# ScalarE and VectorE in program order from the fourth plain step of a fused attention and two-layer MoE kernel

## The chip, the core and the metric

The kernel runs on one core of one Trainium2 chip. The metric is the device time of one execution in microseconds (us). Engines are named as the profile names them: PE (TensorE matmul), PEld (its weight loads), DVE (VectorE), ACT (ScalarE), POOL (GpSimd), SP (SyncE, which here issues DMAs only).

## The reference, cut to what matters

```python
def reference(q, k, v, w_in, w_out, w_gate, w_val, w_out2, rms_g):
    # B=4, H=8, S=576, D=64: local mask for heads 0-3, strided mask for heads 4-7
    x = attention(q, k, v).transpose(0, 2, 1, 3).reshape(2304, 512)
    h = x @ w_in                                # 512 -> 2048
    x = (h - np.tanh(h)) @ w_out                # 2048 -> 512      (MoE1)
    xn = x / np.sqrt(np.mean(x * x, -1, keepdims=True) + 1e-6) * rms_g
    g = xn @ w_gate                             # 512 -> 1536
    val = xn @ w_val
    return (g / (1 + np.exp(-g)) * val) @ w_out2    # 1536 -> 512  (MoE2)
```

The weights arrive as 64-bit floats. The kernel splits each into a high and a low 32-bit part and computes a product as three matmuls (high·high, high·low, low·high).

## The kernel before, in words

**Stages.** Attention runs first, with MoE1 overlapped; MoE1 goes through the 2304 tokens in five groups. Its last outputs stand in four accumulators `ps_x`; `evac_x` (L885) scales them on ACT into tiles `xe` (L890) and ACT's queue writes these to the DRAM tensor `x2d` (L896). MoE2 then treats the first R0 = 256 tokens in 12 "plain" steps (the loop at L1376, f = 0 to 11) and the other 2048 by Strassen products (class `Stage`, L1071), which need seven inputs `xt1` to `xt7`, built by `conv` (L1019) while the plain steps run. Everything asked about here lies in the plain steps and the some 10 us ahead of them.

**One plain step.** `pe_gv` (L923) runs 24 matmuls of 128x256 on TensorE: 12 for gate into a bank of PSUM, 12 for val into another. ACT takes silu of the gate (L937), VectorE multiplies by val (L938, tile `s`), ACT makes the high half of `p` (L940), VectorE the low half (L941). Two steps later `pe_o` (L944) multiplies `p` by w_out2: 6 matmuls of 128x512 into two accumulators `ps_x`. In every third step gate and val take two banks of the `ps_x` pool, in the others two of two banks tagged "h" and "m"; so three steps have banks at a time.

**Weights.** While the plain steps run, the last of w_gate and w_val are decoded. For one tile of 128x512: SP loads it (`raw`, L175, three buffers); ACT computes `ct` (L184) and `ca` (L186); VectorE merges them into `ct` (L196); ACT casts the high half `w` (L203); VectorE subtracts for the low half of `w` (L207). `Stream.step` (L230) does L184, L186, L196 for one weight and L203, L207 for the one before it. `Store.plain` (L338) stores merged tiles to DRAM (`v`, L343), `Store.to` (L346) the split ones. `Decode` on POOL later builds Strassen's weight combinations from `v` (L285, L302).

**Strassen inputs.** `conv(m)`: for m = 5, 6, 7, 4 VectorE first forms a difference `tr` (L1027); for m = 1, 2, 3 it needs none. Then ACT casts the high half (L1046) and VectorE subtracts for the low half (L1047). `preps` (L907) is a generator: it norms x, then yields one `conv` at a time.

**Order of the work.** A scheduler orders each engine's instructions with a timeline of its own, so the loop's program order is only a starting point; `tc.manual_schedule` makes the listed engines keep program order. Before, it holds for SP from MoE1's fourth group on, and for PE and SP after the plain steps. Each engine executes its list in that order.

## Time and profile before

| what | value |
|---|---|
| time, median of 3 runs | 887.31 us (885.79 to 887.9) |
| time of the profiled execution | 887.14 us |
| its span, first to last instruction | 885.3 us |
| mean granted TensorE clock | 0.990 |
| PE, DVE, ACT, POOL busy | 865.6, 626.1, 413.7, 247.6 us |
| the largest wait of PE between 455 and 545 us | 4.94 us, at 469.51 us |

The profiled execution takes 1.8 us more than its span. Times in the timeline count from the span's start. A matmul's busy time in the trace runs from its start to its modelled end, so a lone one shows more than the distance at which matmuls follow each other. In a view of instruction groups, "idle before" is the time in which the engine stood still just ahead of them, and the name behind the arrow is what ended it. The granted clock is 1.00 at 2.4 GHz and 0.50 at 1.2 GHz; a stretch with both shows a value between.

### The profile page before, as it was taken

What the parts mean: (1) busy time and instruction counts of PE and PEld (TensorE: products, weight loads), DVE (VectorE), ACT (ScalarE), POOL (GpSimd) and SP (SyncE); (2) the same over time, 40 slices, a digit from 0 to 9 for tenths busy, and PEclk for the clock granted to TensorE, in tenths of its full rate; (3) what the DMA queues carried; (4) which work ended last, traced back from release to release, by engine and by line L of the source; (5) the groups of instructions that cost most, each with busy time, mean ns of one, the idle gap of its engine ahead of it and who ended that gap; (6) DMA issues with size and microseconds to landing.
All of it is one profiled execution on the core that took longest, in us unless ns stands there. A gap on an engine that the chain in (4) does not pass through costs nothing.

```text
span 885.3 us, 14070 instructions
## 1 busy us (share of the span) xinstructions
PE 865.6 (98%) x5091; PEld 723.4 (82%) x5091; DVE 626.1 (71%) x1290; ACT 413.7 (47%) x916; POOL 247.6 (28%) x309
## 2 busy tenths in 40 slices
PE   7999999999999999999997999999999999999998
PEld 4888888888998887888887977888888888888886
DVE  5999778888779887657779845469688553435544
ACT  6887633323543333778657544533325324322230
POOL 0000057694366853000000449956200000000000
PEclk7999999999999999999999999999999999999999
DMA  9965224221313000889976889866661289544002
GB/s 302 367 221 180 76 75 157 98 63 36 116 55 110 25 19 26 330 311 366 412 262 226 302 304 410 329 239 214 212 216 48 82 315 348 182 147 140 1 1 95
DMA packets 63749, 164.12 MB, mean 185 GB/s; under 512 B 10112, under 2 KB 21760, under 8 KB 63680
## 3 DMA queue, kind: packets, MB, share of 16 engines
q1 hardware_dynamic: 62528, 162.18, 52.2%
q10 hardware_dynamic: 1152, 1.05, 0.3%
q8 instruction: 40, 0.66, 0.3%
q14 instruction: 29, 0.24, 0.1%
HBM read 119.16 MB, written 44.04 MB: 184 GB/s over the span
## 4 chain that ended last, share of the span: by engine, by line
PE 60%; DVE 9%; POOL 7%; issue 2%; DMA 2%; ACT 1%; ACTq 0%; SPq 0%; DVEq 0%; POOLq 0%
PE ps_pr L150 21%; PE ps_o L150 15%; PE ps_x L150 9%; PE ps_h L150 9%; POOL pr L674 5%; DVE so L714 4%; PE ps_q L150 4%; PE ps_m L150 1%; POOL pr L707 1%; DMA raw<-in_w_val_dram 1%; DVE tg L859 1%; DVE g L870 1%; DMA x2d<-xe 1%; DVE sm L450 0%; DMA sq<-in_q_str_dram 0%
## 5 line engine op out<-in xcount | busy, mean ns | idle before, releaser
L150 PE MATMUL ps_h<-xs,w 128*128 128x512 f32 (+1 forms) x984 | 214.3, 366 | 0.7 <-DVE tg L859 0.7
L150 PE MATMUL ps_x<-g,w 128*128 128x512 f32 (+1 forms) x984 | 214.1, 366 | 0.0
L150 PEld LDWEIGHTS ps_h<-xs,w 128*128 128x128 f32 x984 | 169.7, 190 | 30.5 <-DVE tg L859 1.2
L150 PEld LDWEIGHTS ps_x<-g,w 128*128 128x128 f32 x984 | 168.5, 189 | 30.3 <-ACT g L865 0.4
L150 PE MATMUL ps_pr<-xt,wt 128*128 128x512 f32 x576 | 137.0, 390 | 0.5 <-DVE s L1096 0.5
L150 PE MATMUL ps_o<-wt,p 128*128 128x512 f32 x576 | 135.9, 389 | 0.0
L150 PEld LDWEIGHTS ps_pr<-xt,wt 128*128 128x128 f32 x576 | 107.9, 188 | 23.6 <-DVE s L1096 0.9
L150 PEld LDWEIGHTS ps_o<-wt,p 128*128 128x128 f32 x576 | 108.1, 188 | 22.4
L674 POOL TENSOR_TENSOR pr<-sk,sq 128x256 f32<-128x256 f32 (+2 forms) x101 | 83.1, 857 | 132.2 <-DMA sq<-in_q_str_dram 127.8
L865 ACT CAST g<-tg 128x512 fp32r<-128x512 f32 (+1 forms) x82 | 46.5, 567 | 101.2 <-DVE tg L859 100.9
L1117 ACT COPY u<-ps_pr 128x512 f32<-128x512 f32 x72 | 41.9, 587 | 102.8 <-PE ps_pr L150 102.8
L707 POOL TENSOR_TENSOR pr<-sv,se 128x288 f32<-128x288 f32 (+12 forms) x104 | 69.7, 691 | 57.4 <-DVE so L714 19.8
L1169 DVE SCALAR_TENSOR_TENSOR osum<-ps_o,osum 128x512 f32<-128x512 f32 x80 | 54.8, 687 | 26.6 <-PE ps_o L150 25.9
L714 DVE TENSOR_REDUCE so<-pr 128x16 f32<-128x272 f32 (+11 forms) x104 | 64.8, 651 | 8.9 <-POOL pr L707 8.6
L302 POOL TENSOR_TENSOR ws<-wa 128x256 f32<-128x256 f32 x24 | 20.4, 872 | 179.6 <-DVE w L207 155.6
L150 PE MATMUL ps_pr<-xt,wo 128*128 128x512 f32 x288 | 67.4, 389 | 0.0
L150 PEld LDWEIGHTS ps_pr<-xt,wo 128*128 128x128 f32 x288 | 54.1, 188 | 11.2
L870 DVE TENSOR_TENSOR g<-tg,g 128x512 fp32r<-128x512 f32 (+1 forms) x82 | 55.2, 674 | 10.4 <-ACT g L865 9.8
L859 DVE SCALAR_TENSOR_TENSOR tg<-ps_h,tg 128x512 f32<-128x512 f32 (+1 forms) x82 | 50.5, 617 | 15.8 <-ACT tg L854 15.8
L196 DVE SCALAR_TENSOR_TENSOR ct<-ca,ct 128x512 uint32<-128x512 uint32 x68 | 47.5, 706 | 18.9 <-ACT ca L186 18.4
L854 ACT ACTIVATE tg<-ps_h 128x512 f32<-128x512 f32 (+1 forms) x82 | 44.2, 540 | 35.5 <-PE ps_h L150 35.4
L679 DVE TENSOR_REDUCE sc<-pr 128x4 f32<-128x256 f32 (+2 forms) x101 | 43.7, 436 | 12.1 <-POOL pr L674 11.6
(123 smaller groups left out, 1041.1 us busy)
## 6 DMA issues: line engine op xcount, KB each, us to landing
wt<-w SPq DMA_DIRECT2D x84, 512.0 KB, 4.6
w<-w SPq DMA_DIRECT2D x36, 512.0 KB, 6.2
raw<-in_w_out_dram SPq DMA_DIRECT2D x28, 512.0 KB, 6.1
w<-wo SPq DMA_DIRECT2D x24, 512.0 KB, 7.1
raw<-in_w_in_dram SPq DMA_DIRECT2D x16, 512.0 KB, 9.2
raw<-in_w_gate_dram SPq DMA_DIRECT2D x12, 512.0 KB, 7.0
raw<-in_w_val_dram SPq DMA_DIRECT2D x12, 512.0 KB, 7.4
v<-ct SPq DMA_DIRECT2D x24, 256.0 KB, 5.3
```

Source lines behind the costliest of these rows:

```text
L150: nc.tensor.matmul(out_, lhsT, rhs, start=start, stop=stop, skip_group_check=True)
L196: nc.vector.scalar_tensor_tensor(out=t, in0=self.a.bitcast(U32), scalar=3, in1=t, op0=ALU.logical_shift_left, op1=ALU.bitwise_or)
L674: nc.gpsimd.tensor_tensor(out=pr, in0=self.k[:, a:e, :], in1=self.q[:, c - c0:c - c0 + 1, :].to_broadcast([128, e - a, D]), op=ALU.mult,)
L679: pend.append(lambda: nc.vector.tensor_reduce(out=s[:, c - c0, a:e], in_=pr, axis=AX.X, op=ALU.add))
L707: nc.gpsimd.tensor_tensor(out=pr, in0=self.v[:, 0:c + 1, a:e], in1=self.e[:, c - c0, 0:c + 1].unsqueeze(2).to_broadcast([128, c + 1, e - a ...
L714: pend.append(lambda: nc.vector.tensor_reduce(out=o[:, c - g0, a:e], in_=pr.rearrange("l c d -> l d c"), axis=AX.X, op=ALU.add))
L854: nc.scalar.activation(out=t, in_=h_of[g, f, a], func=ACTF.Tanh, scale=WS)
L859: nc.vector.scalar_tensor_tensor(out=t, in0=h_of.pop((g, f, a)), scalar=WS, in1=t, op0=ALU.mult, op1=ALU.subtract)
L865: nc.scalar.copy(out=t[:, 0], in_=t_of[g, f, a])
L870: nc.vector.tensor_tensor(out=t[:, 1], in0=t_of.pop((g, f, a)), in1=t[:, 0].bitcast(F32), op=ALU.subtract)
L1117: nc.scalar.copy(out=u, in_=x[kd])
L1169: nc.vector.scalar_tensor_tensor(out=o, in0=ps, scalar=WS, in1=o, op0=ALU.mult, op1=ALU.add)
```

## The change

Five edits, all around the plain steps.

1. `Store.plain`: the eight `v` stores that come after MoE1 go to ACT's queue rather than SP's.
2. `evac_x` for the last group: the first two accumulators are moved into one pair tile of their own and stored together; the other two go to two tiles of another pool. Two stores of 128x2x256 and four of 128x256 take the place of eight of 128x256, and no tile is used twice.
3. `pe_gv`: gate and val of a step take the two halves of one bank, and six banks are taken in turn (two of "h", two of "m", two of the `ps_x` pool), so six steps have banks at a time.
4. The pools of the plain steps are opened in another order, so other buffers take over the memory that `xe` had.
5. From f = 3 to the loop's end ACT and VectorE keep program order. A step's order is: `Stream.step`s for its weights, the `v` stores, the matmuls, silu, `s`, `p`, then one Strassen input (two at f = 3, none before). Before, the generator was advanced three times a step from f = 0, and the scheduler placed what it issued.

```diff
@@ -340,7 +340,8 @@
                 w = w2[w2_order[self.m]]
                 if w.kind != "out2":
                     p, i = divmod(w.f, 2)
-                    nc.sync.dma_start(out=pairs[p].plain[2 * (w.kind == "val") + i], in_=w.b)
+                    queue = nc.sync if cvt.name == "cvt" else nc.scalar
+                    queue.dma_start(out=pairs[p].plain[2 * (w.kind == "val") + i], in_=w.b)
                 self.m += 1
 
         def to(self, n):
@@ -883,19 +884,32 @@
             evac_x(g)
 
     def evac_x(g):
-        queue = nc.sync if g < NG - 1 else nc.scalar
+        last = g == NG - 1
+        if last:
+            pair = ghl.tile([128, 2, 512], F32, tag="g0", name="xe")
         for c in range(4):
-            pool, tag = (gp, nth("tg", 3)) if g == NG - 1 else (cvt, ("ca", "ct")[c % 2])
-            t = pool.tile([128, 512], F32, tag=tag, name="xe")[:, :width[g]]
+            if last:
+                t = pair[:, c % 2] if c < 2 else gp.tile([128, 512], F32, tag=f"tg{c - 2}", name="xe")
+            else:
+                t = cvt.tile([128, 512], F32, tag=("ca", "ct")[c % 2], name="xe")[:, :width[g]]
             nc.scalar.mul(out=t, in_=xacc[g][c][:, :width[g]], mul=WS)
+            if last and c == 0:
+                continue
             for k, j in enumerate(groups[g]):
                 dst, src = x2d[c * 128:c * 128 + 128, :], t[:, SUB * k:SUB * k + SUB]
                 rs = runs(j)
                 b, t0, n, _ = rs[0]
-                if len(rs) == 1:
-                    queue.dma_start(out=dst[:, b * S + t0:b * S + t0 + n], in_=src)
+                if last and c == 1:
+                    nc.scalar.dma_start(
+                        out=x2d[:256, b * S + t0:b * S + t0 + n].rearrange("(c p) t -> p c t", p=128),
+                        in_=pair[:, :, SUB * k:SUB * k + SUB],
+                    )
+                elif last:
+                    nc.scalar.dma_start(out=dst[:, b * S + t0:b * S + t0 + n], in_=src)
+                elif len(rs) == 1:
+                    nc.sync.dma_start(out=dst[:, b * S + t0:b * S + t0 + n], in_=src)
                 else:
-                    queue.dma_start(
+                    nc.sync.dma_start(
                         out=dst.rearrange("p (b t) -> p b t", b=B)[:, :, t0:t0 + n],
                         in_=src.rearrange("p (b t) -> p b t", b=B),
                     )
@@ -922,11 +936,9 @@
 
     def pe_gv(j, f):
         r, n = [], R0
-        for kd, pool, tag in (("gate", ps_h, "h"), ("val", ps_m, "m")):
-            if f % 3 == 2:
-                ps = bank_x("ps_" + tag)[:, :n]
-            else:
-                ps = pool.tile([128, 512], F32, tag=nth(tag, 2), name="ps_" + tag)[:, :n]
+        bank = (bank_h, bank_m, bank_h, bank_m, bank_x, bank_x)[f % 6]("ps_h")
+        for k, kd in enumerate(("gate", "val")):
+            ps = bank[:, k * n:k * n + n]
             w, x = w2[kd, f].t, xn[j]
             seq = [(a, e, c) for c in range(4) for a, e in ((0, 0), (0, 1), (1, 0))]
             for i, (a, e, c) in enumerate(seq):
@@ -1366,28 +1378,33 @@
     for k, m in enumerate((3, 7)):
         xt[m] = late[:, 2048 * k:2048 * k + 4 * HT].rearrange("p (e c t) -> p e c t", e=2, c=2)
     poolB = ExitStack()
+    tmp[3] = (poolB.enter_context(tc.tile_pool(name="rawb", bufs=3, reuse_waits="tile")), "raw")
     tmp[0] = poolB.enter_context(tc.tile_pool(name="tmp", bufs=4, reuse_waits="tile"))
+    pb = poolB.enter_context(tc.tile_pool(name="pb", bufs=2, reuse_waits="tile"))
+    cvt = poolB.enter_context(tc.tile_pool(name="cvt2", bufs=2, reuse_waits="tile"))
     tmp[1] = None
-    cvt = poolB.enter_context(tc.tile_pool(name="cvt2", bufs=2, reuse_waits="tile"))
     tmp[2] = cvt
-    tmp[3] = (poolB.enter_context(tc.tile_pool(name="rawb", bufs=3, reuse_waits="tile")), "raw")
-    pb = poolB.enter_context(tc.tile_pool(name="pb", bufs=2, reuse_waits="tile"))
 
     for f in range(FB):
+        if f == 3:
+            order = ctx.enter_context(ExitStack())
+            order.enter_context(tc.manual_schedule(engines={mybir.EngineType.Activation, mybir.EngineType.DVE}))
         if f == FB - 4:
             pairs[0].fetch((0, 1))
         st2.to(max(3 * (f + 2), N1 + (len(w2_order) - N1) * (f + 1) // (FB - 2)))
         store.plain(st2.i - 1)
         store.to(st2.i - 6)
         pe_gv(0, f)
-        for _ in range(3 if f < FB - 2 else 40):
+        for _ in range((f >= 3) + (f == 3) if f < FB - 2 else 40):
             next(pg, None)
         decode.to(max(0, min(8, 8 * (f - 4) // 6)))
-        if f > 1:
+        if f >= 2:
             pe_o(0, f - 2)
-    pe_o(0, FB - 2)
+    for f in range(FB - 2, FB - 1):
+        pe_o(0, f)
     store.plain(len(w2_order))
     store.to(len(w2_order))
+    order.close()
     ctx.enter_context(tc.manual_schedule(engines={mybir.EngineType.PE, mybir.EngineType.SP}))
 
     def second():
```

What moves can be read from the instruction lists. Names carry the number of their buffer, and `p_5961` means the `p` of one step. **ACT, around the ninth gate weight, before:**

```order
L203 CAST w_5949<-ct_5939 128x512
L940 CAST p_5928<-s_5925 128x256
L940 CAST p_5984<-s_5981 128x256
L940 CAST p_6026<-s_6023 128x256
L184 ACTIVATE ct_6043<-raw_5937,colf_58 128x512
L186 ACTIVATE ca_6045<-raw_5937 128x512
L1046 CAST xt4_5708<-tr_5820 128x1024
L203 CAST w_5993<-ct_5944 128x512
L937 ACTIVATE s_6087<-ps_h_6061 128x256
L937 ACTIVATE s_6136<-ps_h_6110 128x256
L937 ACTIVATE s_6204<-ps_h_6178 128x256
L203 CAST w_6055<-ct_6043 128x512
```

The casts of weights stand close together, silu and `p` go in threes. **ACT, the same place, after:**

```order
L203 CAST w_5927<-ct_5917 128x512
L344 DMA v4_1_163<-ct_5917 128x512
L949 ACTIVATE s_5958<-ps_h_5933 128x256
L952 CAST p_5961<-s_5958 128x256
L1058 CAST xt5_5703<-tr_5964 128x1024
L203 CAST w_5974<-ct_5922 128x512
L344 DMA v4_3_165<-ct_5922 128x512
L949 ACTIVATE s_6003<-ps_h_5978 128x256
L952 CAST p_6006<-s_6003 128x256
L1058 CAST xt6_5704<-tr_6009 128x1024
L184 ACTIVATE ct_6027<-raw_5915,colf_58 128x512
L186 ACTIVATE ca_6029<-raw_5915 128x512
```

Behind gate 9's cast now come the silu and `p` of step f = 4, a Strassen cast of 128x1024, and only then the cast of val 9, `w_5974`. From the row of `ct_6027` the pattern begins anew: two steps f = 4 and f = 5 take one gate and one val weight, and so do f = 6 and 7, 8 and 9.

**VectorE, the same place, before:**

```order
L941 TENSOR_TENSOR p_5928<-s_5925,p_5928 128x256
L941 TENSOR_TENSOR p_5984<-s_5981,p_5984 128x256
L941 TENSOR_TENSOR p_6026<-s_6023,p_6026 128x256
L196 SCALAR_TENSOR_TENSOR ct_6043<-ca_6045,ct_6043 128x512
L1047 TENSOR_TENSOR xt4_5708<-tr_5820,xt4_5708 128x1024
L207 TENSOR_TENSOR w_5993<-ct_5944,w_5993 128x512
L938 SCALAR_TENSOR_TENSOR s_6087<-ps_m_6074,s_6087 128x256
L938 SCALAR_TENSOR_TENSOR s_6136<-ps_m_6123,s_6136 128x256
```

**VectorE, after:**

```order
L207 TENSOR_TENSOR w_5927<-ct_5917,w_5927 128x512
L950 SCALAR_TENSOR_TENSOR s_5958<-ps_h_5933,s_5958 128x256
L953 TENSOR_TENSOR p_5961<-s_5958,p_5961 128x256
L1039 TENSOR_TENSOR tr_5964<-x2_5239 128x1024
L1059 TENSOR_TENSOR xt5_5703<-tr_5964,xt5_5703 128x1024
L207 TENSOR_TENSOR w_5974<-ct_5922,w_5974 128x512
L950 SCALAR_TENSOR_TENSOR s_6003<-ps_h_5978,s_6003 128x256
L953 TENSOR_TENSOR p_6006<-s_6003,p_6006 128x256
L1039 TENSOR_TENSOR tr_6009<-x2_5239,tr_5964 128x1024
L1059 TENSOR_TENSOR xt6_5704<-tr_6009,xt6_5704 128x1024
L196 SCALAR_TENSOR_TENSOR ct_6027<-ca_6029,ct_6027 128x512
```

The low half of a weight had stood between Strassen's large instructions as its input came. Now the difference `tr_5964` follows the low half of `p_5961`, and the low half of the val weight `w_5974` and then `s_6003` follow the Strassen subtraction.

**TensorE, after, from the first matmuls of gate 9 (f = 9) to those of gate 10:**

```order
L150 MATMUL ps_h_6211<-xn_5193,w_5927 128x256 x12
L150 MATMUL ps_x_5846<-w_5325,p_5961 128x512 x2
L150 MATMUL ps_x_5847<-w_5325,p_5961 128x512 x2
L150 MATMUL ps_x_5846<-w_5325,p_5961 128x512
L150 MATMUL ps_x_5847<-w_5325,p_5961 128x512
L150 MATMUL ps_h_6211<-xn_5193,w_5974 128x256 x12
L150 MATMUL ps_x_5846<-w_5426,p_6006 128x512 x2
L150 MATMUL ps_x_5847<-w_5426,p_6006 128x512 x2
L150 MATMUL ps_x_5846<-w_5426,p_6006 128x512
L150 MATMUL ps_x_5847<-w_5426,p_6006 128x512
L150 MATMUL ps_h_6253<-xn_5193,w_6039 128x256 x12
```

Gate 10, val 10 and two more outputs follow in the same pattern, so that from gate 9's first matmul to gate 11's first there are 48 of 128x256 and 24 of 128x512; the outputs in between are those of steps 4 to 7. Ahead of these rows, from the end of MoE1's matmuls on, TensorE's list has 168 of 128x256 (steps 1 and 3 to 8) and 24 of 128x512 (the outputs of steps 0 to 3), so it runs four to five steps ahead of its outputs; before, three.

## Rows read from the trace of the kernel before

**Rows 1.** The page: span, and busy time of each engine.
```profile
span 885.3 us, 14070 instructions
...
PE 865.6 (98%) x5091; PEld 723.4 (82%) x5091; DVE 626.1 (71%) x1290; ACT 413.7 (47%) x916; POOL 247.6 (28%) x309
```

**Rows 2.** What TensorE waits for, 455 to 545 us; columns as in the second row.
```profile
engine line waited for: us in total, times, longest us
PE ps_h L150 <- ACT s L937: 4.9, 1, 4.9
PE ps_x L150 <- ACT p L940: 1.0, 1, 1.0
PE ps_pr L150 <- DVE s L1096: 0.5, 1, 0.5
PE ps_m L150 <- ACT w L203: 0.3, 1, 0.3
PE ps_m L150 <- DVE w L207: 0.2, 1, 0.2
```

**Rows 3.** Timeline of TensorE around 470 us; columns as in the second row.
```profile
start us, us, engine line op out<-in xcount [idle before <-releaser]
...
460.40 1.35 PE L150 MATMUL ps_m<-xn,w 128*128 128x256 f32 x10
461.59 2.91 PE L150 MATMUL ps_x<-g,w 128*128 128x512 f32 x12
464.34 0.40 PE L150 MATMUL ps_m<-xn,w 128*128 128x256 f32 x2
...
466.47 3.04 PE L150 MATMUL ps_m<-xn,w 128*128 128x256 f32 x24
474.45 3.74 PE L150 MATMUL ps_h<-xn,w 128*128 128x256 f32 x18 [4.94 <-ACT s L937]
```

**Rows 4.** Stretches of 5 and 10 us: busy time by engine, granted clock, DMA share.
```profile
core 0: us, PE busy (x) PEld busy (x) DVE busy (x) ACT busy (x) POOL busy (x), PEclk, DMA share, GB/s
...
470.00:475.00 5.00, 0.55 (x2) 0.55 (x3) 4.90 (x9) 2.84 (x7) 0.00 (x0) 0.90 0.17 59
475.00:480.00 5.00, 5.00 (x35) 5.00 (x34) 4.78 (x7) 5.00 (x7) 0.00 (x0) 0.75 0.49 161
480.00:485.00 5.00, 5.00 (x40) 4.82 (x40) 5.00 (x7) 5.00 (x10) 0.00 (x0) 1.00 0.96 320
...
500.00:510.00 10.00, 10.00 (x66) 9.11 (x65) 6.25 (x8) 3.88 (x9) 9.11 (x11) 1.00 0.99 346
```

**Rows 5.** Timeline of ScalarE, 467 to 475 us.
```profile
467.76 0.33 ACTq L896 DMA_DIRECT2D x2d<-xe  x1
468.13 0.60 ACT L890 ACTIVATE xe<-ps_x 128x512 f32<-128x512 f32 x1 [2.21 <-DMA x2d<-xe]
468.76 1.05 ACTq L896 DMA_DIRECT2D x2d<-xe  x2
472.16 0.76 ACT L184 ACTIVATE ct<-raw,colf 128x512 uint32<-128x512 uint16 x1 [3.43 <-DMA x2d<-xe]
472.82 0.66 ACT L186 ACTIVATE ca<-raw 128x512 f32<-128x512 f32 x1
473.38 0.75 ACT L184 ACTIVATE ct<-raw,colf 128x512 uint32<-128x512 uint16 x1
474.03 0.90 ACT L937 ACTIVATE s<-ps_h 128x256 f32<-128x256 f32 x3
```

**Rows 6.** ScalarE's groups by shape, 470 to 530 us: busy, mean ns, idle before.
```profile
L184 ACT ACTIVATE ct<-raw,colf 128x512 uint32<-128x512 uint16 x10 | 7.5, 766 | 9.2 <-DMA raw<-in_w_val_dram 5.0 <-DMA x2d<-xe 3.4 <-DMA raw<-in_w_gate_dram 0.5
L186 ACT ACTIVATE ca<-raw 128x512 f32<-128x512 f32 x10 | 6.6, 664 | 0.0
L203 ACT CAST w<-ct 128x512 fp32r<-128x512 f32 x10 | 6.2, 617 | 3.7 <-DVE ct L196 3.6
L940 ACT CAST p<-s 128x256 fp32r<-128x256 f32 x12 | 4.5, 404 | 7.5 <-DVE s L938 5.5 <-PE ps_x L150 1.8
L1046 ACT CAST xt<-tr 128x1024 fp32r<-128x1024 f32 x4 | 4.1, 1039 | 0.0
L937 ACT ACTIVATE s<-ps_h 128x256 f32<-128x256 f32 x12 | 3.8, 370 | 0.0
```

**Rows 7.** VectorE's groups by shape, same stretch.
```profile
L207 DVE TENSOR_TENSOR w<-ct,w 128x512 fp32r<-128x512 f32 x10 | 8.5, 854 | 1.4 <-ACT w L203 1.4
L196 DVE SCALAR_TENSOR_TENSOR ct<-ca,ct 128x512 uint32<-128x512 uint32 x10 | 7.5, 749 | 4.9 <-ACT ca L186 4.9
L941 DVE TENSOR_TENSOR p<-s,p 128x256 fp32r<-128x256 f32 x12 | 6.3, 560 | 1.2 <-ACT p L940 1.2
L1047 DVE TENSOR_TENSOR xt<-tr,xt 128x1024 fp32r<-128x1024 f32 x4 | 4.8, 1210 | 0.0
L938 DVE SCALAR_TENSOR_TENSOR s<-ps_m,s 128x256 f32<-128x256 f32 x12 | 4.5, 412 | 2.6 <-PE ps_m L150 2.6
...
L1027 DVE TENSOR_TENSOR tr<-x 128x1024 f32<-128x1024 f32 x2 | 2.4, 1214 | 0.0
```

**Rows 8.** Timeline of VectorE, 489 to 496 us, before POOL runs.
```profile
489.17 1.21 DVE L1047 TENSOR_TENSOR xt<-tr,xt 128x1024 fp32r<-128x1024 f32 x1
490.31 0.68 DVE L207 TENSOR_TENSOR w<-ct,w 128x512 fp32r<-128x512 f32 x1
490.91 0.68 DVE L196 SCALAR_TENSOR_TENSOR ct<-ca,ct 128x512 uint32<-128x512 uint32 x1
491.51 1.07 DVE L938 SCALAR_TENSOR_TENSOR s<-ps_m,s 128x256 f32<-128x256 f32 x3
...
495.45 1.08 DVE L941 TENSOR_TENSOR p<-s,p 128x256 fp32r<-128x256 f32 x3
```

**Rows 9.** Timeline of ScalarE at the end of the plain steps.
```profile
515.87 0.77 ACT L184 ACTIVATE ct<-raw,colf 128x512 uint32<-128x512 uint16 x1 [3.22 <-DMA raw<-in_w_val_dram]
```

## The prediction

> **What bounds the kernel now.** I read the page first: TensorE is busy 865.6 of 885.3 us [rows 1], so a change here can only take away waits of TensorE or add some. The view of its waits shows where they are: between 455 and 545 us five, 6.9 us in sum, 4.94 of them one stall [rows 2]. The timeline of TensorE gives its place, 469.51 us, and its sequel: the 18 matmuls of 128x256 behind it took 3.74 us, where 24 took 3.04 us before it [rows 3]. The stretches give the reason: the granted clock was 0.90 and then 0.75, so for part of the time at the lower of the two levels, and again 1.00 from 480 us [rows 4]. At full clock these matmuls follow each other every 0.119 us (ten from 460.40 to 461.59) and those of 128x512 every 0.229 us (twelve from 461.59 to 464.34) [rows 3]; 18 x 0.119 plus a tail of 0.18 us (3.04 less 24 x 0.119) is 2.32 us, so the clock cost 1.42 us.
>
> TensorE waited for a silu, and ScalarE's timeline shows why that was late: an `xe` eviction waited 2.21 us and a `ct` 3.43 us, both for a store of `xe` to `x2d`, with the three silus behind them in the list [rows 5].
>
> **The change part by part.**
>
> *Evictions and pools (edits 2 and 4).* Each of the four `xe` has a place of its own, and the next pools' first tiles do not lie where `xe` was. Both waits of [rows 5] lose their cause; what remains on ScalarE is four evictions of 0.60 us and six DMA issues of 0.33 to 0.5 us. *Banks (edit 3).* With six steps' banks TensorE does not ask for silu 0 after three steps, but its list goes on with step 1 and most of step 6 (46 matmuls of 128x256, 5.5 us) ahead of the first output. Either part takes the 4.94 us and the 1.42 us away. The small waits near 519 to 522 us, 0.3 + 0.2 + 1.0 = 1.5 us [rows 2], also go or are replaced by what comes below; the 0.5 us for `s` of L1096 I leave where it is, since it belongs to Strassen's first product. Gain: 4.9 + 1.4 + 1.5 = 7.8 us, the most that these rows hold.
>
> *The `v` stores on ScalarE (edit 1).* Eight issues of some 0.4 us (0.33 for one, 1.05 for two, [rows 5]) move from SP's queue to ScalarE's; their cost is in the chain below. SP loses as much, but its loads of `raw` wait for free buffers, so I count nothing there.
>
> *Program order (edit 5).* This is the part that costs. From f = 3 on each instruction of ScalarE and VectorE waits for all that stand ahead of it in the list. I followed the printed lists with the durations of the trace. An instruction of ScalarE starts about 0.1 us before its forerunner's end (`ca` 0.66 us after a `ct` of 0.76 [rows 5]), so in a row `ct` takes 0.66, `ca` 0.56, a weight's cast 0.52, a Strassen cast 0.95 us, from means of 0.766, 0.664, 0.617 and 1.04 [rows 6]; silu 0.37, `p` 0.40 and an issue 0.40 stand in full. VectorE takes 0.68 for a merge or a weight's low half and some 0.41 for `s` or the low half of `p` while POOL rests [rows 8], 1.21 for a difference or a Strassen subtraction [rows 7]. Hand-overs between engines I take at 0.04 us.
>
> - Step f = 4: `ct`, `ca`, `ct`, `ca`, cast, issue: 0.66 + 0.56 + 0.66 + 0.56 + 0.52 + 0.40 = 3.4. Then silu, `s` on VectorE, `p`: 1.25. Then ScalarE has nothing to do until VectorE has made the low half of `p` and the difference: 0.41 + 1.21 + hand-overs = 1.7. Then the Strassen cast, 0.95. Sum 7.2 us (rounded down).
> - Step f = 5: the cast of val 9, issue and silu hide under VectorE, which has the Strassen subtraction of step 4 (1.21), the low half of val 9 (0.68) and `s` (0.41) to do: `p` can start 2.3 us after the cast of val 9 does. Then 0.40 + 1.7 + 0.95. Sum 5.3 us.
> - Step f = 6: as f = 4, but its Strassen input needs no difference: 7.2 - 1.7 = 5.5 us. Step f = 7: as f = 5, 5.3 us.
>
> From the low half of gate 9 (step f = 4) to that of gate 11 (at the same place of step f = 8) that is 7.2 + 5.3 + 5.5 + 5.3 = **23.3 us**. TensorE's own work between the first matmuls of these two gates is 48 x 0.119 + 24 x 0.229 = **11.2 us**. If it comes to gate 9 no later than this weight, it stands 12.1 us in sum. Does it? MoE1's matmuls end near 466 us, as before (the last twelve `ps_x` end near 464.5 [rows 3], a few more stand behind them); 168 x 0.119 + 24 x 0.229 = 25.5 us later it is 491.6. On ScalarE: evictions from 465.5, their issues to 470.5, three silus (one waits for step 1's matmuls, 466.2 + 48 x 0.119 = 471.9) and three `p` to 474.0, two `ct` and `ca` for step 7's weights to 476.4, a wait of some 1.7 for VectorE, which ends the norm of x first, two casts and two issues to 480.0; step f = 3 with two Strassen casts 8.0, to 488.0; then the four decodes and the cast of gate 9, 3.0, and its low half 0.7: 491.8 us. So both come at once, and none of the 12.1 us is covered. They fall on val 9 and gates 10 and 11, about 2, 4 and 4 us with the matmuls at lower clock in between; val 11 comes 5.3 us after gate 11, for which TensorE has 12 matmuls of gate 11, 12 of Strassen's first products and an output of six: 1.4 + 4.1 = 5.5 us, just enough.
>
> *The clock.* In this trace it fell after a wait of 4.94 us and not after one of 1.0 us [rows 2, 4]. Between them no row tells. The two stalls of 3.5 to 4 us are nearer to the first, so I take the fall for both: one is within the 12.1 us (it delays TensorE's way to gate 11, and the weights don't care), the other adds 1.4 us. Bounds: nothing is added if it doesn't fall after the last, and 2.8 if that fall lasts twice as long.
>
> Sum: -7.8 + 12.1 + 1.4 = **+5.7 us** against the profiled execution's 887.14, which is 0.2 under the median: **892.8 us**. 0.3% is 2.7 us, about what a measurement of this kernel can tell from no change: slower.
>
> One rule is weighed here. What the row shows: a `ct` that waited 3.43 us for a store held back three silus [rows 5], two of whose banks TensorE had filled before. The Trainium skill says the same of these engines in general ("TensorE: Matmul & The Clock Gate", Architectural detail): ScalarE and VectorE are strict first-in, first-out queues. By this the bubbles above (1.7 at f = 4, 5 and 7, some 1.0 at each odd step for `s`, and 0.9 to 1.3 for `s` at each even one) are paid by all behind them, 23.3 us in sum. Were ready instructions let past, the four steps would take ScalarE's own work alone, 14.8 us (3.4 + 0.3 + 0.3 + 0.95, and 0.52 + 0.4 + 0.3 + 0.3 + 0.95, both twice), TensorE would stand 3.6, and the sum would be -7.8 + 3.6 = -4.2 us, 882.9. The row decides for the queue.
>
> **The rivals.**
>
> *The chain keeps pace (faster).* If the four steps took 11.2 us or less per TensorE's need, or TensorE came to gate 9 later than I think, only the gain stays: 887.14 - 7.8 = 879.3 us; with half of the 12.1 us covered and no fall of the clock, 885.4. It decides at 19.0 us for the four steps instead of 23.3 (7.8 + 11.2); below 16.3 the kernel is faster by over 0.3%. For it: before, both engines did the same work in this stretch with waits of TensorE of 1.5 us, and ScalarE is busy only 3.88 of 10 us from 500 to 510 us [rows 4]; TensorE is released earlier. Against it: the list lets no work be moved into these idle times, and VectorE's 1.21 us instructions stand on ScalarE's way five times in the four steps (three differences, two subtractions). The Trainium skill speaks for this rival ("Perfetto Trace Analysis", Matmuls): independent matmul groups should rotate through different PSUM banks so that one's evacuation overlaps the next's matmuls. No stall of the rows for banks alone is left for that after 480 us, though.
>
> *About even.* Half of the bubbles are hidden, or the clock stays up and VectorE's work is a little shorter: 885 to 889.8 us.
>
> *A weight comes late from DRAM (slower still).* ScalarE's last val weight waited 3.22 us for its load [rows 9], with the DMA engines busy 0.99 of the time [rows 4]. In the fixed list a late `raw` holds back silu, `p` and the Strassen input as well, and a `v` store that waits on ScalarE's queue does so too. One such wait in the chain adds 3.2 us: 896.0. VectorE is dearer beside POOL: 0.854 and 0.560 us for the low halves of weight and `p` [rows 7] rather than 0.68 and 0.41, which adds 0.15 x 4 + 0.17 x 4 = 1.3 us to the chain.
>
> *The change does not do what it says.* The printed lists show the program order and the six banks, so this has no chance worth a number.
>
> **How the numbers follow.** Forecast (890 to 894.5) 0.50; slower still 0.10; about even 0.14; faster 0.26, of which some 0.10 below 881. So faster 0.26, same 0.14, slower 0.60. The range leaves out the best tenth of the faster case and what lies above a late weight with its dearer VectorE (892.8 + 3.2 + 1.3 = 897.3): 881 to 897. The forecast's own range is 890 (no second fall of the clock, -1.4, and a chain shorter by 6 in 100, another -1.4) to 894.5 (VectorE dearer beside POOL, +1.3, and rounding).
>
> **What would show it.** Right: the stall of 4.94 us and the fall of the clock at 474 us gone; new stalls of TensorE between 494 and 515 us, of 3 us and more, in matmuls of `ps_h` for `w` of L207 on VectorE; ScalarE waiting for VectorE's `tr` about 1.7 us ahead of four Strassen casts; the plain steps ending some 5 us later. Wrong: no stall above 1 us after 480 us, or the old stall still there, or the stalls waiting for `raw` rather than for `w`.

## The result, and the profile after

| | before | after |
|---|---|---|
| median, runs of this comparison | 886.63 us (4 runs) | 898.36 us (897.02 to 899.84, 4 runs) |
| span of the profiled execution | 885.3 us | 897.1 us |
| mean granted clock | 0.990 | 0.986 |

The ratio is 1.012, with a 95% interval of 1.0096 to 1.0145: slower by 10.6 us, 8.5 to 12.9 (the two medians are 11.7 us apart, the two profiled executions 11.8). The direction was forecast; the size was not, and the time lies above the range.

The page of the changed kernel, as in [rows 1]:

```profile
span 897.1 us, 14054 instructions
...
PE 869.2 (97%) x5091; PEld 725.0 (81%) x5091; DVE 634.2 (71%) x1290; ACT 413.3 (46%) x916; POOL 247.6 (28%) x309
```

TensorE's waits between 440 and 600 us, as in [rows 2], the two largest groups:

```profile
engine line waited for: us in total, times, longest us
PE ps_h L150 <- ACT w L203: 8.8, 3, 4.1
PE ps_h L150 <- DVE w L207: 3.3, 3, 2.1
```

Its timeline, as in [rows 3], shows each of them; the wait in brackets lies ahead of the row's first matmul:

```profile
495.21 0.50 PE L150 MATMUL ps_h<-xn,w 128*128 128x256 f32 x2 [1.03 <-ACT w L203]
496.55 2.43 PE L150 MATMUL ps_h<-xn,w 128*128 128x256 f32 x10 [0.84 <-DVE w L207]
...
505.03 0.80 PE L150 MATMUL ps_h<-xn,w 128*128 128x256 f32 x2 [4.10 <-ACT w L203]
507.93 2.50 PE L150 MATMUL ps_h<-xn,w 128*128 128x256 f32 x10 [2.10 <-DVE w L207]
...
519.84 0.50 PE L150 MATMUL ps_h<-xn,w 128*128 128x256 f32 x2 [3.65 <-ACT w L203]
520.66 2.50 PE L150 MATMUL ps_h<-xn,w 128*128 128x256 f32 x10 [0.32 <-DVE w L207]
```

The stall at 469.5 us is gone. Six new waits, 12.0 us in sum, stand at val 9, gate 10 and gate 11, where the forecast had put 12.1 us. The stretches, as in [rows 4], add what the forecast had not:

```profile
core 0: us, PE busy (x) PEld busy (x) DVE busy (x) ACT busy (x) POOL busy (x), PEclk, DMA share, GB/s
...
475.00:480.00 5.00, 5.00 (x35) 4.59 (x34) 4.39 (x8) 3.00 (x6) 0.00 (x0) 1.00 0.89 293
...
495.00:500.00 5.00, 3.95 (x15) 3.52 (x16) 3.42 (x6) 1.95 (x5) 0.91 (x2) 0.67 0.99 269
500.00:505.00 5.00, 0.93 (x4) 0.39 (x2) 3.23 (x3) 3.00 (x6) 4.92 (x6) 0.84 0.98 397
505.00:510.00 5.00, 2.87 (x11) 2.57 (x12) 4.22 (x5) 1.96 (x4) 4.92 (x5) 0.50 1.02 407
510.00:515.00 5.00, 5.00 (x23) 4.38 (x22) 4.47 (x5) 0.86 (x3) 4.92 (x6) 0.63 0.82 316
...
520.00:525.00 5.00, 4.68 (x19) 4.11 (x20) 3.36 (x6) 2.32 (x5) 0.00 (x0) 0.66 0.37 134
```

TensorE now runs through 475 to 480 us at full clock, but from 495 us on the granted clock falls again and again. A value of 0.67 over 5 us is 3.3 us at the lower level; the five low rows make 17 us, where the kernel before had 3.5 us in all of the plain steps ((1 - 0.75) x 2 x 5 + (1 - 0.90) x 2 x 5 from [rows 4]).

ScalarE's timeline gives the chain, since the casts of gate 9, val 9, gate 10, val 10 and gate 11 are the rows at 489.76, 494.54, 504.37, 509.56 and 519.18:

```profile
489.76 0.60 ACT L203 CAST w<-ct 128x512 fp32r<-128x512 f32 x1
...
494.54 0.61 ACT L203 CAST w<-ct 128x512 fp32r<-128x512 f32 x1
...
503.15 0.76 ACT L184 ACTIVATE ct<-raw,colf 128x512 uint32<-128x512 uint16 x1 [2.00 <-DMA w<-w]
...
504.37 0.61 ACT L203 CAST w<-ct 128x512 fp32r<-128x512 f32 x1
...
508.30 0.41 ACT L952 CAST p<-s 128x256 fp32r<-128x256 f32 x1 [3.04 <-DVE s L950]
...
509.56 0.61 ACT L203 CAST w<-ct 128x512 fp32r<-128x512 f32 x1
...
519.18 0.60 ACT L203 CAST w<-ct 128x512 fp32r<-128x512 f32 x1
```

VectorE's low halves of gates 9 and 11 start at 490.50 and 519.92, **29.4 us** apart, not 23.3:

```profile
490.50 0.69 DVE L207 TENSOR_TENSOR w<-ct,w 128x512 fp32r<-128x512 f32 x1
...
501.52 1.21 DVE L196 SCALAR_TENSOR_TENSOR ct<-ca,ct 128x512 uint32<-128x512 uint32 x1
504.50 1.70 DVE L196 SCALAR_TENSOR_TENSOR ct<-ca,ct 128x512 uint32<-128x512 uint32 x1 [1.77 <-ACT ca L186]
506.13 1.75 DVE L207 TENSOR_TENSOR w<-ct,w 128x512 fp32r<-128x512 f32 x1
507.80 0.41 DVE L950 SCALAR_TENSOR_TENSOR s<-ps_h,s 128x256 f32<-128x256 f32 x1
...
513.47 2.31 DVE L1039 TENSOR_TENSOR tr<-x 128x1024 f32<-128x1024 f32 x1
...
519.92 0.68 DVE L207 TENSOR_TENSOR w<-ct,w 128x512 fp32r<-128x512 f32 x1
```

POOL ran from 499.09 us, and its last row of that stretch ends at 516.9:

```profile
499.09 1.43 POOL L302 TENSOR_TENSOR ws<-wa 128x256 f32<-128x256 f32 x2 [157.17 <-PE ps_h L150]
...
513.24 3.68 POOL L286 TENSOR_TENSOR wo<-ws,wo 128x512 fp32r<-128x512 f32 x2
```

Beside POOL two merges of 128x512 took 1.21 and 1.70 us where they take 0.69 without it, the low half of gate 10 1.75 and not 0.68, a Strassen difference 2.31 and not 1.21. `s`, which has one input in PSUM, stays at 0.41.

### The profile page after: what moved, and what is told of

It reads as the page before. It is cut to its first block, busy times and chain, and to the rows that moved or that the text cites. A ratio compares the mean times of both kernels' runs of the same rounds, so it can differ in the third digit from the quotient of the medians.

```text
span 897.1 us, 14054 instructions
## 1 busy us (share of the span) xinstructions
PE 869.2 (97%) x5091; PEld 725.0 (81%) x5091; DVE 634.2 (71%) x1290; ACT 413.3 (46%) x916; POOL 247.6 (28%) x309
## 4 chain that ended last, share of the span: by engine, by line
PE 48%; DVE 12%; POOL 7%; DMA 7%; ACT 4%; issue 3%; SPq 0%; ACTq 0%; DVEq 0%; POOLq 0%
PE ps_pr L150 20%; PE ps_o L150 14%; POOL pr L675 5%; PE ps_x L150 5%; PE ps_h L150 5%; DVE so L715 4%; PE ps_q L150 4%; DMA w<-w 2%; DMA raw<-in_w_val_dram 2%; DMA raw<-in_w_out_dram 1%; POOL pr L708 1%; ACT ct L184 1%; DVE tg L860 1%; ACT ca L186 1%; DVE g L871 1%
## 5 line engine op out<-in xcount | busy, mean ns | idle before, releaser
L150 PEld LDWEIGHTS ps_pr<-xt,wo 128*128 128x128 f32 x288 | 54.1, 188 | 11.2
L150 PE MATMUL ps_h<-xn,w 128*128 128x256 f32 x288 | 41.9, 303 | 12.0 <-ACT w L203 8.8
```

The lines of the kernel that those rows point to most:

```text
L150: nc.tensor.matmul(out_, lhsT, rhs, start=start, stop=stop, skip_group_check=True)
```

## The experiments

Eighteen kernels. Since the first 400 us of a profiled execution differ from run to run by up to 5 us (the 2900th matmul, ahead of all that was changed, starts between 402.3 and 407.3 us), traces are compared by TensorE's n-th matmul, counted from 0: its start less that of the 2900th, against the same in the kernel before. Minus is a lead. A ratio below is always to the kernel before, run in the same comparison, with its 95% interval. Worked out from the matmul rows of each trace:

```
matmul  before  after   e1    e2     e4    e6    e9    e15   e17
3240    478.9   -6.0   -6.3  +0.3   -5.9  -6.4  -5.9  -6.5  -6.5
3320    490.4   -6.0   -6.3  +0.9   -5.9  -6.4  -5.9  -6.0  -6.0
3400    502.0   -6.7   -0.8  +0.5   -6.3  -5.0  -6.6  -4.3  -4.5
3440    508.1   +6.8   -1.1  +1.1   +3.1  -4.9  +2.8  -4.3  -4.2
3480    515.4  +12.4   -1.2  +8.6   +7.0  +0.4  +3.2  -3.6  +2.0
3560    533.5  +11.3   -1.6  +8.2   +7.0  -0.1  +9.9  -3.4  +3.9
5090    881.3  +13.1   -0.7 +10.2   +7.5  +1.9 +10.7  -1.8  +4.9
```

The order of the two shapes of matmul differs between the kernels, so at some rows a kernel has done more or less work than the one before: at 0.119 and 0.229 us each the difference is up to 2.0 us (e2 at the 3480th; 1.2 for the changed kernel there). At the 2900th, 3240th, 3560th and 5090th matmul all kernels have done the same work, and at the 3320th the changed kernel has too.

The changed kernel has a lead of 6 us until 494 us and loses 17.3 us between the 3320th and the 3560th matmul. Its waits there are 12.04 us against 1.49 before: 10.55 of the 17.3. The rest, some 6.7 us, I put down to the lower clock: of the 17 us at that level TensorE worked for about 13, and ten matmuls of 128x256 took 2.43 us there (row 496.55) where they had taken 1.35 at full clock [rows 3].

### The order, and POOL beside it (e1 to e4)

My theory after the result: the fixed order's chain is the cause as forecast, and VectorE beside POOL made it longer. Rivals: the other edits, or the order only together with them.

**e1**, the change without edit 5:

```diff
-        if f == 3:
-            order = ctx.enter_context(ExitStack())
-            order.enter_context(tc.manual_schedule(engines={mybir.EngineType.Activation, mybir.EngineType.DVE}))
...
-    order.close()
...
-        for _ in range((f >= 3) + (f == 3) if f < FB - 2 else 40):
+        for _ in range(3 if f < FB - 2 else 40):
```

> The changed kernel without its fifth edit: the scheduler orders ScalarE and VectorE, three Strassen inputs are offered a step from f = 0, the other four edits stay. Theory (the program order alone is what costs): the stall of 4.94 us and the fall of the clock stay gone, no new stall over 1.5 us comes in their place, 879 to 883 us. Rival (the one-bank steps, the pools or the v stores on ScalarE's queue cost): stalls of 3 us and more between 490 and 525 us stay, 893 us or more.

Measured: 887.35 us, ratio 1.0001 (0.9987 to 1.0014). Edit 5 is what costs, and the other four edits gain nothing in sum, which I had not expected. The table shows why: their 6.3 us are there at 485 us and most of them are given back by 502. TensorE's timeline and the stretches (columns as above) of e1:

```profile
494.68 1.80 PE L150 MATMUL ps_h<-xn,w 128*128 128x256 f32 x12 [1.82 <-DVE w L207]
```

```profile
480.00:490.00 10.00, 9.65 (x67) 8.64 (x65) 10.00 (x13) 10.00 (x17) 0.00 (x0) 1.00 0.80 292
490.00:500.00 10.00, 7.82 (x41) 6.75 (x41) 10.00 (x17) 7.11 (x14) 3.58 (x2) 0.83 1.02 331
```

VectorE is busy 10.00 of 10 us in both stretches. TensorE comes sooner to weights that come no sooner (counted from the 2900th matmul, seven low halves in a row start 2.3 to 3.5 us later than before), waits 1.82 us for one, and loses more to the clock that falls behind it (0.83).

**e2**, the kernel before with edit 5 alone (against before):

```diff
+        if f == 3:
+            order = ctx.enter_context(ExitStack())
+            order.enter_context(tc.manual_schedule(engines={mybir.EngineType.Activation, mybir.EngineType.DVE}))
...
-        for _ in range(3 if f < FB - 2 else 40):
+        for _ in range((f >= 3) + (f == 3) if f < FB - 2 else 40):
...
+    order.close()
```

> The kernel before with the fifth edit alone (program order from f = 3 and one Strassen input a step). Theory: the old stall of 4.94 us stays and the chain of the fixed order comes on top, with gate 11's low half some 25 to 29 us behind gate 9's: 895 to 905 us. Rival (the order costs only together with six banks or the stores on ScalarE): within 3 us of before.

897.65 us, ratio 1.0116 (1.0095 to 1.0137), as expected. Its first stall stays, at 5.25 us, and a second of 5.78 us comes at 518 us.

**e3**, val weights split a step earlier:

```diff
-        st2.to(max(3 * (f + 2), N1 + (len(w2_order) - N1) * (f + 1) // (FB - 2)))
+        st2.to(max(3 * (f + 2), N1 + (len(w2_order) - N1) * (f + 1) // (FB - 2)) + (f in (4, 6, 8)))
```

> The changed kernel, with the split of val 9, 10 and 11 one step earlier (steps f = 4, 6 and 8), so that their casts stand ahead of silu, p and the Strassen input. If the place of the val weights' cast behind a Strassen input is what costs: the waits of TensorE ahead of val weights (1.9, 2.1 and 0.3 us) go and those ahead of gates 10 and 11 shrink too, about 888 us. If the length of the whole chain from gate to gate is what costs: the val waits go, but gates 10 and 11 still come 12 and 14 us apart, and the waits move to them: 894 to 898 us.

900.24 us, ratio 1.014 (1.0124 to 1.0156). The waits for val are gone, those for gates 10 and 11 grew to 5.2 and 6.3 us, and a wait of 2.34 us for a `p` came in: it is the chain's length that counts. The time lies above what either theory gave.

**e4**, POOL's work out of the way (the combinations and their loads come behind the last step; POOL starts at 514 us):

```diff
-        decode.to(max(0, min(8, 8 * (f - 4) // 6)))
+        decode.to(8 if f == FB - 1 else 0)
```

> The changed kernel, with POOL's decode of the first pair (and its loads) issued at the last plain step rather than from f = 5 on. If VectorE beside POOL and the loads in SP's queue made the chain longer than I had summed (29.4 us from gate 9's to gate 11's low half instead of 23.3): it comes down to 23 to 25 us, and the waits for weights to some 12 us with TensorE's matmuls. Rival (the durations have nothing to do with POOL): it stays at 28 us or more. The time itself can go either way, since Strassen's combinations come later: 890 to 908 us.

893.30 us, ratio 1.007 (1.0054 to 1.0087). ScalarE's casts of gate 9, val 9, gate 10, val 10 and gate 11, then VectorE's merge of val 10 and low half of gate 10, at the same place as the rows at 504.50 and 506.13 above:

```profile
489.24 0.61 ACT L203 CAST w<-ct 128x512 fp32r<-128x512 f32 x1
...
494.02 0.61 ACT L203 CAST w<-ct 128x512 fp32r<-128x512 f32 x1
...
501.75 0.60 ACT L203 CAST w<-ct 128x512 fp32r<-128x512 f32 x1
...
503.59 0.41 ACT L952 CAST p<-s 128x256 fp32r<-128x256 f32 x1 [0.97 <-DVE s L950]
...
504.86 0.62 ACT L203 CAST w<-ct 128x512 fp32r<-128x512 f32 x1
...
512.64 0.61 ACT L203 CAST w<-ct 128x512 fp32r<-128x512 f32 x1
```

```profile
501.88 0.69 DVE L196 SCALAR_TENSOR_TENSOR ct<-ca,ct 128x512 uint32<-128x512 uint32 x1 [0.51 <-ACT ca L186]
502.48 0.69 DVE L207 TENSOR_TENSOR w<-ct,w 128x512 fp32r<-128x512 f32 x1
```

Gate 9 to gate 11 takes 512.64 - 489.24 = **23.4 us**, within 0.1 of the sum in the prediction. By pieces, after against e4 (and the prediction's steps): gate 9 to val 9 4.8 and 4.8 (4.8); val 9 to gate 10 9.8 and 7.7 (7.8); gate 10 to val 10 5.2 and 3.1 (3.1); val 10 to gate 11 9.6 and 7.8 (7.8). The three pieces that grew are those in which POOL ran. e4's time fits as well: it is 6.0 us above the median of its own before (887.33), where the prediction's sum gave +5.7.

e4 moved POOL's loads together with its work, but it is not the transfers that draw out VectorE's instructions: with POOL at rest and the DMA engines busy 0.90 to 1.03 of the time (e4, 485 to 505 us) no merge or low half took over 0.70 us and no Strassen instruction over 1.23. The loads did add a part of their own. In the changed kernel `ct` of val 10 waited 2.00 us (row 503.15): the load of its `raw`, issued at 494.42 behind four loads for POOL, landed at 503.07 us. In e8 below that wait did not come, and the distance was 28.8 us, which would leave some 0.6 of the 6.0 us to it; e8's rows beside POOL are not the same, so this is no more than an indication.

### Which order, which inputs, which queue (e5 to e11)

**e5**, program order with three Strassen inputs a step from f = 0:

```diff
-        for _ in range((f >= 3) + (f == 3) if f < FB - 2 else 40):
+        for _ in range(3 if f < FB - 2 else 40):
```

> The changed kernel with program order from f = 3 kept, but the Strassen inputs offered three a step from f = 0 as before, so that they stand ahead of the weights of the last steps instead of between them. Theory (what costs is the Strassen input between two weights, with VectorE's 1.2 us instructions that ScalarE waits for, not program order as such): no wait for gates 10 and 11 above 2 us; a wait for the weights of steps 7 to 9 instead, since some 13 us of VectorE's work now stand ahead of them; 885 to 892 us. Rival (program order costs whatever it orders): 895 us or more.

895.88 us, ratio 1.0101 (1.0059 to 1.0143). The rival's number came true: waits of 0.3 to 1.8 us at six of the nine weights from gate 7 to gate 11, 9.1 us in sum. My theory that only the inputs between two weights cost fell here.

**e6**, no program order, one input a step:

```diff
-        if f == 3:
-            order = ctx.enter_context(ExitStack())
-            order.enter_context(tc.manual_schedule(engines={mybir.EngineType.Activation, mybir.EngineType.DVE}))
...
-    order.close()
```

> The changed kernel without program order, but with the Strassen inputs offered one a step from f = 3 on as the change does. Theory (the scheduler moves them to where it likes, so the offer alone does little): within 2 us of the kernel without the fifth edit, 885 to 889 us. Rival (the offer, not the order, is what costs): 893 us or more.

889.99 us, ratio 1.0025 (1.0008 to 1.0042). The offer alone moves little. By the table it keeps a lead of 5 us until the 3440th matmul and has lost it by the 3480th, beside POOL.

**e7**, e1 with e4's late decode (against e1):

```diff
-        decode.to(max(0, min(8, 8 * (f - 4) // 6)))
+        decode.to(8 if f == FB - 1 else 0)
```

> The changed kernel without its fifth edit and with POOL's decode of the first pair at the last plain step. If VectorE beside POOL is what took back the gain of the first four edits: 880 to 883 us. If that gain is lost ahead of POOL's work, to weights that VectorE, busy without a break from 475 us on, cannot decode sooner: within 2 us of before, 885 to 889 us, with the wait near 493 us as before.

894.47 us, ratio 1.0081 (1.0053 to 1.0108), above both numbers. The lead is lost near 493 us as in e1, long before POOL has begun, and behind the plain steps TensorE waits 1.74 and 2.28 us for POOL's `wo` of L286.

**e8**, the change with the `v` stores on SP:

```diff
-                queue = nc.sync if cvt.name == "cvt" else nc.scalar
+                queue = nc.sync
```

> The changed kernel without its first edit: the v stores stay on SP's queue. Theory (an issue on ScalarE's queue costs at most its 0.4 us, and mostly lies beside an instruction that still runs): 895 to 899 us. Rival (stores that wait on ScalarE's queue lengthen the chain by some 1 us each): 888 to 892 us.

897.06 us, ratio 1.011 (1.0076 to 1.0143): inside the change's own interval. In this order the stores' queue is not what costs. (The trace of the changed kernel has ten of these stores on ScalarE's queue, not eight.)

**e9** and **e10**, program order with the inputs moved behind most of the weights:

```diff
-        for _ in range((f >= 3) + (f == 3) if f < FB - 2 else 40):
+        for _ in range((f == 4) + (f == 7) + (f == 8) + (f == 9) if f < FB - 1 else 40):
```

for e9, and for e10

```diff
-        for _ in range((f >= 3) + (f == 3) if f < FB - 2 else 40):
+        for _ in range((f == 8) + 2 * (f == 9) + (f == 10) if f < FB - 1 else 40):
```

> The changed kernel with program order kept from f = 3, POOL's decode as it is, and only the places of the seven Strassen inputs changed: one each at f = 4, 7, 8 and 9, and the three that Strassen uses last behind the twelfth step's p. Theory (the Strassen inputs between the weights, drawn out by POOL, are the cost): without them two steps take ScalarE some 6.7 us against TensorE's 8.4, so no wait above 1.5 us before the last weight, and the lead of 6 us over the kernel before that the first four edits give at 490 us is kept in part: 881 to 886 us. Rival (program order loses by VectorE beside POOL whatever stands where): waits of 3 us for gate or val 10 and 11 stay, 890 us or more.

> As the run before, but no Strassen input ahead of f = 8: one at f = 8, two at f = 9, one at f = 10, three behind the last p. Theory: the waits in the plain steps are as small or smaller, but the first Strassen products can come to wait for their inputs near 520 us; 881 to 887 us.

895.48 us, ratio 1.0099 (1.0081 to 1.0117), and 900.95 us, ratio 1.0145 (1.0119 to 1.0171). Both theories (881 to 886 and 881 to 887 us) fell; e9's rival, 890 us or more, came true, with 5.6 us of waits at gate 10 and 0.3 at gate 11. With the inputs gone from between the weights, ScalarE's list stopped for other things that came late (e9's timeline):

```profile
490.04 0.38 ACT L949 ACTIVATE s<-ps_h 128x256 f32<-128x256 f32 x1 [1.97 <-DMA v<-ct]
...
499.30 0.75 ACT L184 ACTIVATE ct<-raw,colf 128x512 uint32<-128x512 uint16 x1 [3.18 <-DMA raw<-in_w_val_dram]
```

A `v` store of gate 9 that waits in ScalarE's list holds a silu for 1.97 us, a `raw` that is late holds all behind it for 3.18 us, and Strassen waits 2.76 us for ScalarE's `u` (e9, 534 us), which I put down to the three inputs put last. Every order written out by hand here lost 0.7% or more (after, e2, e3, e4, e5, e8, e9, e10); without it the same edits lie between -0.4 and +0.8%.

**e11**, no program order, inputs offered later (against e6):

```diff
-        for _ in range((f >= 3) + (f == 3) if f < FB - 2 else 40):
+        for _ in range((4 <= f <= 7) if f < FB - 1 else 40):
```

> The first four edits, no program order, the Strassen inputs offered one a step from f = 4 to 7 and three behind the loop's last step. The scheduler still puts three inputs early. Theory: as with one offered a step from f = 3 (1.94 us lost against before in the profiled execution), but some 2.5 us of VectorE's work less ahead of gates 10 and 11; 883 to 888 us.

892.96 us, ratio 1.0069 (1.005 to 1.0088), a miss. ScalarE waited 3.57 us for a difference `tr` at 508 us. VectorE had no pause ahead of it: from 504.10 us it made a Strassen subtraction, a low half in 1.21 us and this difference in 1.75, all beside POOL.

### Where the gain of the other edits went (e12 to e18)

**e12** and **e13**: e6 and e1, each with POOL's decode from f = 8:

```diff
-        decode.to(max(0, min(8, 8 * (f - 4) // 6)))
+        decode.to(max(0, min(8, 8 * (f - 7) // 4)))
```

> The first four edits, no program order, one Strassen input a step from f = 3, and POOL's decode of the first pair from f = 8 instead of f = 5. With the decode from f = 5 the lead of 6 us over the kernel before was still 4.9 us at 504 us and gone at 517 us. Theory (VectorE beside POOL slows the last weights, and that took the lead): with POOL some 10 us later 2 to 5 us of it stay, 882 to 885 us. Rival (the lead is lost to the amount of VectorE's work, or Strassen then waits for POOL): 887 us or more.

> The first four edits, no program order, three Strassen inputs a step from f = 0, and POOL's decode of the first pair from f = 8. Here the lead was lost near 493 us, ahead of POOL's first instruction, to weights that came late from a VectorE busy without a break. Theory: moving POOL changes nothing of that, and the time stays within 2 us of before, 885 to 889 us. Rival (POOL's loads or work took the lead here too): 880 to 884 us.

892.28 us, ratio 1.0039 (1.0024 to 1.0055), and 890.60 us, 1.0035 (1.0015 to 1.0056). Both lose the lead by 500 us, ahead of POOL (in e12 to a `p` that was 2.48 us late at 493 us; the scheduler had ordered the steps anew, which I take for the reason), and 4 to 5 us more from the 3480th to the 3560th matmul, where Strassen waits for POOL's `wo` (2.27 us in e12, 0.72 and 2.27 in e13). I read this so, which no run proves: the lead goes to the amount of VectorE's work, and POOL has no free place, since sooner it slows VectorE and later TensorE waits for it.

**e14**: e6 with the last three inputs offered in the last step (against e6):

```diff
-        for _ in range((f >= 3) + (f == 3) if f < FB - 2 else 40):
+        for _ in range(2 * (f == 3) + (4 <= f <= 5) if f < FB - 1 else 40):
```

> The first four edits, no program order, Strassen inputs 1, 2, 5 and 6 offered at f = 3 to 5 and the last three behind the last step; the scheduler then puts the seventh behind the weights of step 10. Theory: VectorE's 2.4 us for that input no longer stand ahead of the last weights beside POOL, so 2 to 3 us of the lead that one offered a step lost from 504 to 517 us stay, 884 to 886 us. Rival (the weights and p are late by POOL and the loads alone): 887 us or more.

888.16 us, ratio 1.0001 (0.9985 to 1.0017): no gain against the kernel before, as the rival had it.

**e15**: edits 1, 2 and 4 without the six banks. **e16**: the six banks alone (before with edit 3). Against e1, e15 is

```diff
-        bank = (bank_h, bank_m, bank_h, bank_m, bank_x, bank_x)[f % 6]("ps_h")
-        for k, kd in enumerate(("gate", "val")):
-            ps = bank[:, k * n:k * n + n]
+        for kd, pool, tag in (("gate", ps_h, "h"), ("val", ps_m, "m")):
+            if f % 3 == 2:
+                ps = bank_x("ps_" + tag)[:, :n]
+            else:
+                ps = pool.tile([128, 512], F32, tag=nth(tag, 2), name="ps_" + tag)[:, :n]
```

and e16 is the same lines the other way, against before.

> The kernel before with the evictions, the pools and the v stores on ScalarE's queue of the change (edits 1, 2 and 4), without its six banks and without program order. If the store that ScalarE waited for is enough: the wait of 4.94 us shrinks to under 2 us and the clock stays up at 475 us. If TensorE has to run ahead as well: 3 us and more of it stay. Either way VectorE sets the end of the stretch: 885 to 889 us.

> The kernel before with the six banks of the change alone (edit 3). If running ahead is enough: TensorE has 46 matmuls of 128x256 (5.5 us) more to do ahead of the first output and waits less than 1 us at 470 us. Rival: silu is late all the same and the wait only moves, to the first output near 475 us. Either way 885 to 890 us.

e15: **884.05 us, ratio 0.9961 (0.9943 to 0.9980)**, faster than both kernels. e16: 890.74 us, ratio 1.0036 (1.0018 to 1.0054). TensorE's timeline of e15, then of e16:

```profile
466.87 3.04 PE L150 MATMUL ps_m<-xn,w 128*128 128x256 f32 x24
469.75 3.04 PE L150 MATMUL ps_h<-xn,w 128*128 128x256 f32 x24
472.63 0.76 PE L150 MATMUL ps_m<-xn,w 128*128 128x256 f32 x5
...
493.91 1.45 PE L150 MATMUL ps_h<-xn,w 128*128 128x256 f32 x10 [1.15 <-DVE w L207]
```

```profile
480.12 5.44 PE L150 MATMUL ps_h<-xn,w 128*128 128x256 f32 x26 [6.44 <-DVE s L936]
```

With the stores of `xe` out of the way TensorE does not stand at 470 us at all, though it has three steps' banks only. With six banks alone it stands 6.44 us, one step (24 matmuls) further on than before: silu is late all the same (477.16 us), and so is the `s` that frees a bank. The 26 matmuls behind it run mostly at the lower clock (0.52 from 480 to 485 us) and take 5.44 us, where at full clock they would take some 3.3.

**e17**: e15 with the `v` stores on SP (edits 2 and 4 alone), the edit of e8 made in e15. **e18**: e15 with one input offered a step, as in e6:

```diff
-        for _ in range(3 if f < FB - 2 else 40):
+        for _ in range((f >= 3) + (f == 3) if f < FB - 2 else 40):
```

> The kernel before with edits 2 and 4 alone (evictions and pools; three steps' banks, v stores on SP, the scheduler's order). With edit 1 as well it took 0.39% less than before. If evictions and pools are what gives that: 883 to 886 us, the wait of 4.94 us gone. If the v stores on ScalarE's queue gave part of it: 886 us or more.

> Edits 1, 2 and 4 with one Strassen input offered a step from f = 3 instead of three from f = 0. Theory: fewer of VectorE's large instructions ahead of the weights of steps 8 and 9, where 1.15 us were lost, but more of them beside POOL: within 2 us of the version with three a step, 882 to 887 us. Rival: more lead kept, 881 us or less.

890.84 us, ratio 1.0044 (1.0026 to 1.0061), and 888.57 us, 1.0009 (0.9991 to 1.0026). e18 lies 1.6 us above its range: one input a step is not better here. Up to the 3440th matmul e15 and e17 are alike in the table, so edits 2 and 4 alone take the stall away; which of the two does was not tried. Then e17 loses 8 us. SP's waits from 460 to 530 us in e17, the largest:

```profile
SPq L344 <- DVE ct L196: 31.3, 6, 10.1
```

and in e15, where SP has no `v` store:

```profile
SPq L175 <- ACT ca L186: 10.4, 2, 9.4
SPq L175 <- DMA x2d<-xe: 8.3, 2, 6.9
```

A store that waits for a merge at the head of SP's queue holds the loads of `raw` behind it. In e15 these loads have no `v` store ahead of them in SP's queue. One such load was issued at 492.71 us in e15 and at 498.11 in e17, and ScalarE's timeline of e17 shows what came of it:

```profile
504.37 0.76 ACT L184 ACTIVATE ct<-raw,colf 128x512 uint32<-128x512 uint16 x1 [4.86 <-DMA raw<-in_w_val_dram]
```

A `p` stands behind this `ct` in ScalarE's list, and TensorE waited 2.28 us for it at 506 us.

## Why the prediction was wrong

- *The stall of 4.94 us and its fall of the clock go:* right; the lead of 6.0 to 6.3 us at the 3240th matmul is their sum. That "either part takes" them was wrong. Evictions and pools do (e15, and e17 without edit 1), the banks do not (e16). That TensorE and the low half of gate 9 come at once, so that nothing of the chain is covered, was right too: 491.2 and 490.5 us.
- *The chain of 23.3 us:* **this term failed.** Its working was right, as e4 shows (23.4), but its durations held for VectorE "while POOL rests", and from 499 to 517 us POOL works. It was 29.4 us. I had the means of VectorE's groups beside POOL in [rows 7] and used them in a rival only, for 1.3 us; they average over both states and hide instructions at 2.5 times the duration. What VectorE loses there ScalarE waits for: behind gate 10's cast its `p` waited 3.04 us for `s` (row 508.30) and 0.97 in e4 (row 503.59), and the 2.07 us between them are what the merge (1.70 for 0.69) and the low half (1.75 for 0.69) ahead of `s` lost.
- *The clock:* mis-sized. I had no row between a wait of 1 us that left it and one of 4.94 that did not. In the runs it fell behind a wait of 1.82 us (e1) and behind two of 1.03 and 0.84 us (after); the changed kernel spent 17 us at the lower level. With TensorE's own work at the lower clock for most of 500 to 515 us this is the way in which the longer chain shows in TensorE, rather than a term on top: -7.8 + (29.4 - 11.2) + 1.4 = +11.8 us against 887.14 is 898.9, and 898.36 was measured. That this comes so near is in part luck: from the 2900th matmul on the profiled execution lost 13.1 us, and the first 404 us, where nothing was changed, took 1.4 us less than before. Of the 13.1, 1.8 us came behind the 3560th matmul and are not explained.
- *The rivals.* "A weight comes late from DRAM" named the two causes that added up (VectorE beside POOL, a late `raw`) at 897.3 us and a chance of 0.10; it came nearest, but with the shares reversed: it gave POOL 1.3 us and the load 3.2, where POOL cost most of the 6.0 to 6.1. "The change does not do what it says" did not apply.
- *The gain:* I took 7.8 us as what the other edits bring when the order is left out of account. Without the order they bring nothing as they stand (e1) and 3.5 us without the six banks (e15: 0.39% of 887). Where e1 loses what e15 keeps can be read: from 490 to 500 us e15's TensorE waited 1.15 us and its clock stayed at 1.00, e1's waited 1.82 and its clock fell (0.83). Why the banks lead to that was not settled: e1 and e15 differ in the scheduler's order of TensorE too.
- *Rules.* The Trainium skill ("SBUF — State Buffer", SBUF: two separate sides) says that VectorE and GpSimd share one pair of ports, which one of them holds for a whole instruction, among VectorE's the ones with two inputs in SBUF. The trace agrees: merge, low half and difference have two and went from 0.69 to as much as 1.70, 0.68 to 1.75 and 1.21 to 2.31 us, `s` with one input in PSUM kept its 0.41. The Trainium skill also says ("DMA: Bandwidth & Descriptors", Issuing engines are not separate DMA queues) that issuing from several engines only saves issue time. e15 and e17 differ: there the other queue was worth some 7 us (the ratios 0.9961 and 1.0044 are 0.8% apart), since a store that waits at the head of SP's queue holds the loads behind it.

## What to carry to other kernels

A chain summed from rows holds only in the company in which the rows were taken: look at which engine starts beside it, and price each instruction from single rows beside that engine, not from a mean over both. In an order written out by hand an engine waits for the latest of many things: no placing of the Strassen inputs that was tried in such an order helped (e5, e9, e10 lost 1% or more), because the engine then stood for the next late thing. A stall that is removed pays only if the work behind it can come sooner too: see first whether an engine there is busy without a break.

## What the runs showed of the hardware that was not expected

- VectorE's instructions with two inputs in SBUF take up to 2.5 times as long beside POOL (0.69 to 1.70 us; others beside it took 1.21), and `s` with one in PSUM takes no longer (0.41).
- The granted clock fell behind a wait of 1.82 us (e1), and behind 1.03 and 0.84 us in two pieces 0.5 us apart (after); behind 0.95 us alone (before), 1.15 us (e15) and 1.71 us (e17, at 521 us) it did not. So the length of one wait alone does not decide it.
- The same instructions ahead of the 2900th matmul took 402.3 to 407.3 us in the profiled executions, so that a difference of 3 us between two traces has to be read from a common matmul on, not from the span's start. The granted clock of the first 30 us goes with it: 0.89 in those that took 402.3 to 404.9 us, 0.66 to 0.83 in those that took 404.8 to 407.3.
